# Attention and routed experts in one kernel: a 96-row last tile, casts and routing moved between slots

## The chip, the cores and the metric

The kernel runs on one core of one Trainium2 chip. The metric is the device time of one execution in microseconds, here the median of three runs: 294.62 us (294.39 to 295.03). A profiled execution records every instruction and is longer (span 307.8 us); its times are read as differences and shares. The engines: PE is TensorE (PEld its weight loads), ACT ScalarE, DVE VectorE, POOL GpSimd, SP SyncE, which starts most of the large transfers.

## The reference

First a linear attention without softmax, then a layer of eight experts of which each row uses one:

```python
kv = np.einsum('bhsd,bhse->bhde', k, v)          # 8 batches, 8 heads, 576 rows, 64 wide
out = np.einsum('bhsd,bhde->bhse', q, kv)
rms = np.sqrt(np.mean(out * out, axis=-1, keepdims=True) + 1e-06)
x = out / rms * g_norm                            # -> rows: N = 8*576 = 4608, D = 512

logits = x @ w_gate                               # E = 8
expert_idx = np.argmax(logits, axis=1)
probs = np.exp(logits - logits.max(-1, keepdims=True))
probs /= probs.sum(-1, keepdims=True) + 1e-09
gate_w = probs[np.arange(N), expert_idx]
for e in range(E):
    mask = expert_idx == e
    h = np.maximum(x[mask] @ w1[e], 0.0)          # w1: 512 x 1024
    out[mask] = gate_w[mask, None] * (h @ w2[e])  # w2: 1024 x 512
```

The inputs are one fixed draw of random numbers.

## The kernel before

It has two parts. The attention part goes through 36 tiles (slots 0 to 35) of 128 rows: a transpose of q, a product with the batch pair's kv matrices into `op`, the mean of squares, the scaling into fp16 rows `xg`. The gate is folded into kv: each batch's kv is copied, transposed (`kvt`) and multiplied with the gate's weights (`kgp`), and the result stands as 16 more columns beside kv, so the logits come out of the same product. Every few tiles a `Route` finds each row's expert and its rank there, and GpSimd scatters the rows by expert into a scratch array in HBM. The rows of experts 0 and 1 known after 22 tiles (up to 384 each, AT = 3 tiles) are gathered back early.

The expert part runs one job per expert: gather the rows, transpose them (`flip`), first layer with relu (`one`), second layer (`two`), scale, put the rows to their places. Every expert has room for CAP rows in CT tiles, and rows above are done in left-over tiles of 128, the first of them as a ninth job, more in a loop at the end that runs only if they exist.

All instructions stand in the order of the program text on their engines; each engine works strictly through its own list.

```python
    CT = 5
    CAP = CT * 128
    AT = 3
    NOV = (N - CAP) // 128
    BIG = 1.0e6
...
    c32[:, 144:144 + CT] = ar[:, None] + 128.0 * np.arange(CT)   # rank of each place in an expert
```

The copies, transposes and gate products of a batch's kv, and the casts of the weights to fp16:

```python
        def kv_copy(b):
            for ip in range(2):
                ps = slice(64 * ip, 64 * ip + 64)
                nc.scalar.copy(
                    kvsb[b % 4][ps, :, ps].rearrange("p (c i) n -> p c i n", c=2),
                    kvst[b][ps, :, 0:128].rearrange("p c (i n) -> p c i n", i=2),
                )

        def kv_t(b):
            kvtp = PSA.tile([128, 4, 128], F32, tag="misc", bufs=1, name="kvtp")
            for t in range(4):
                nc.tensor.transpose(kvtp[:, t, :], kvsb[b % 4][:, t, 0:128], ident)
            kvst[b] = PA.tile([128, 4, 128], F32, tag="kvt", bufs=1, name="kvt")
            nc.scalar.copy(kvst[b], kvtp)

        def kv_gate(b):
            kgp = PSA.tile([128, 4, 16], F32, tag="misc", bufs=1, name="kgp")
            for t in range(4):
                nc.tensor.matmul(
                    kgp[:, t, :], kvst[b][:, t, :], gw[:, t, :, :], start=True, stop=True
                )
            nc.vector.tensor_copy(kvsb[b % 4][:, :, 128:144], kgp)
...
        def half1(self, eng, kk):
            ...
            if eng is nc.scalar:
                eng.activation(self.w1[:, kk, :], st, ACTF.Copy, scale=g2)
            ...
        def half2(self, kk, eng=None):
            copy = nc.scalar.copy if eng is None else eng.tensor_copy
            ...
```

One tile's norm. `rest` is called at the slot's end, after the list `late`:

```python
        def x_norm(s, op):
            ...
            nc.scalar.activation(                  # sq = op^2
                sq.rearrange("p (c i h) n -> p c i (h n)", c=2, i=2),
                oc[:, :, :, 0:128], ACTF.Square,
            )
            ms = PA.tile([128, 8], F32, tag="ms", bufs=3, name="ms")
            nc.vector.reduce_sum(ms, sq, axis=AXX)

            def rest():
                ...
                nc.scalar.activation(lnt, ms, ACTF.Ln, scale=1.0 / 64.0, bias=epsb)
                ...
                nc.scalar.activation(rinv, lnt, ACTF.Exp, scale=-0.5)
                ...                                # DVE: lr = op's logits * rinv
                ...                                # DVE: xg = op * rinv, frees op
```

Routing is in pieces (`first_a`: three VectorE instructions lg, mx, dl; `first_b`: cd, m2, oh; `ranks` on TensorE; `send`; `scatter`). What is done in which slot is written in the lists `mid`, `late` and `last`:

```python
        def pace(s):                               # POOL waits here for tile s's logits
            P, g0, G, r = place(s)
            nc.gpsimd.tensor_copy(tick, lrs[P, g0][:, r, 0, 0:1])
...
        for b in range(1, B):
            f = 9 * (b // 2) + 4 * (b % 2)         # first slot that needs batch b
            ...
            at(late, f - 2, kv_copy, b)
            at(mid, f - 1, kv_t, b)
            at(late, f - 1, kv_gate, b)
...
        groups = [(P, g0, G) for P in range(3) for g0, G in ((0, 4), (4, 5))]
        for P, g0, G in groups + [(3, 0, 4), (3, 4, 3)]:
            rt = Route(P, g0, G)
            s = 9 * P + g0 + G - 1
            if P < 3:
                at(late, s + 1, rt.first_a)
                at(late, s + 2, rt.first_b)
                ...
            else:
                at(last, s, rt.first)
                at(mid, s + 2, rt.ranks)
                at(late, s + 2, rt.send)
                for t in range(G):
                    at(last, (33, 34, 34, 35)[t] if g0 == 0 else 35, rt.scatter, t)
                    if g0 == 0 and t == 3:
                        for u in range(AT):
                            at(last, 35, gather_early, 1, u)
        for t in range(AT):
            at(last, 30 + t, gather_early, 0, t)

        at(last, 19, W[0].stage1)
        at(last, 21, W[0].stage2)
        at(last, 30, W[1].stage_in, PA)
        for kk in range(4):
            at(last, (25, 26, 28, 29)[kk], W[0].half1, nc.scalar, kk)
        for kk in range(2):
            at(last, 31 + 2 * kk, W[0].half2, kk)
...
        for s in range(36):
            op = x_mm(s)
            for fn in mid[s]:
                fn()
            if s + 2 < 36:
                qt = x_qt(s + 2)
            elif s == 34:
                ...                                # slot 34: flips of expert 0's early rows
            rest = x_norm(s, op)
            if s + 2 < 36:
                x_qs(s + 2, qt)
            ...
            for fn in late[s]:
                fn()
            rest()
            for fn in last[s]:
                fn()
```

The expert jobs:

```python
        class Job:
            def __init__(self, xe, w, okm, bgm, views):
                ...
                self.nt = nt = len(xe)
                self.cols = nt * 128
                self.halves = 2 if self.cols > 512 else 1
                ...
            def one(self, ws, f):
                ...
                wd = self.cols // self.halves
                ...
                for kk in range(4):
                    nc.tensor.matmul(
                        self.hp[:, f % 2, 0:wd],
                        self.w.w1[:, kk, f * 128:(f + 1) * 128],
                        self.xt[:, kk, ws * wd:(ws + 1) * wd],
                        start=(kk == 0),
                        stop=(kk == 3),
                    )
                if f % 2:
                    r = f % 4 - 1
                    nc.scalar.activation(
                        self.ht[f // 4][:, r:r + 2, ws * wd:(ws + 1) * wd],
                        self.hp[:, :, 0:wd], ACTF.Relu,
                    )

            def two(self, t):
                banks.reverse()
                yp = PSA.tile([128, D], F32, tag=banks[0], bufs=1, name="yp")
                for f in range(8):
                    nc.tensor.matmul(
                        yp, self.ht[f // 4][:, f % 4, t * 128:(t + 1) * 128],
                        self.w.w2[:, f, :], start=(f == 0), stop=(f == 7),
                    )
                spare.append(spare.pop(0))
                ys = PA.tile(
                    [128, D], F32, tag=spare[0], bufs=5 if spare[0] == "qp" else 2, name="ys"
                )
                nc.vector.tensor_scalar(
                    ys, yp, self.xe[t][:, 514:516].bitcast(F32), None, op0=ALU.mult
                )
                put(self.views[t], self.idx[:, t:t + 1], ys)
```

Experts 0 and 1 have three of their tiles done early, so two are left for their jobs; experts 2 to 7 have five. In the loop over jobs, a job's first layer goes together with the casts of the next expert's W1 on VectorE and the flips of the next expert's rows, and its second layer with the casts of the next W2 on ScalarE; each cast frees the staging buffer for the next 2 MB load:

```python
            for ws in range(job.halves):
                for f in range(8):
                    job.one(ws, f)
            ...
                    step = 8 * ws + f
                    if coming and (step in (1, 5, 7, 11, 13) if n > 1 else f in (1, 3, 5, 6, 7)):
                        next_row(n + 2, coming.pop(0), job, ws, f)
                    if ws == job.halves - 1 and f in (2, 4, 6) and flips:
                        nxt.flip(flips.pop(0))
                    if n > 0 and ws == 0 and f % 2 == 1 and nxt is not None:
                        W[n + 1].half1(nc.vector, f // 2)
                        if f == 7 and n + 2 < len(order):
                            W[n + 2].stage1()
            for kk in range(max(job.nt, 4)):
                if kk < job.nt:
                    job.two(kk)
                if n > 0 and kk < (2 if n == 1 else 4) and nxt is not None:
                    W[n + 1].half2(kk)
                if n > 1 and kk == 3 and n + 2 < len(order):
                    W[n + 2].stage2()
```

Of the kernel before, what the change touches and what calls it, by code (L numbers as in the profile page):

```python
# [11 lines left out]
F32 = mybir.dt.float32  # L12
F16 = mybir.dt.float16
I32 = mybir.dt.int32
ALU = mybir.AluOpType
# [13 lines left out]
def kernel(  # L29
# [11 lines left out]
    nc = tc.nc  # L41

    B, H, S, Dh = 8, 8, 576, 64
    N = B * S
# [2 lines left out]
    F = 1024  # L47
    RW = 516
    CT = 5
    CAP = CT * 128  # L50
    AT = 3
    NOV = (N - CAP) // 128
    BIG = 1.0e6

    nc.scalar.add_instruction(
# [19 lines left out]
    c32 = np.zeros((128, 128 + 8 + 8 + CT + 36 + 1 + 32), np.float32)  # L75
    c32[:, 0:128] = np.eye(128)
    c32[:, 128:136] = 8.0 - np.arange(8)
    c32[:, 136:144] = N * np.arange(8)
    c32[:, 144:144 + CT] = ar[:, None] + 128.0 * np.arange(CT)
    o = 144 + CT  # L80
    for s in range(36):
        for c in range(2):
# [59 lines left out]
    class Weights:  # L142
        def __init__(self, e):
            self.e = e if isinstance(e, bass.DynSlice) else slice(e, e + 1)
# [68 lines left out]
    def put(view, idx, ys):  # L213
        nc.gpsimd.indirect_dma_start(  # L214
            out=view,
            out_offset=IndirectOffsetOnAxis(ap=idx, axis=0),
            in_=ys,
            in_offset=None,
            bounds_check=N - 1,
            oob_is_err=False,  # L220
        )
# [4 lines left out]
    W = [Weights(e) if e != "left" else None for e in order]  # L226
# [4 lines left out]
    with tc.manual_schedule(engines=by_hand):  # L231
# [5 lines left out]
        for n in range(4):  # L237
            t = PA.tile([128, 4, 144], F32, tag=f"kvs{n}", name=f"kvs{n}")
# [218 lines left out]
        class Early:  # L457
# [28 lines left out]
            def one(self, m, tag):  # L486

                hp = PSA.tile(
                    [128, 2, 512], F32, tag=tag, bufs=2 if tag == "op" else 1, name="hp"
                )  # L490
                for f in range(2):
                    for kk in range(4):
                        nc.tensor.matmul(  # L493
                            hp[:, f, 0:AT * 128],
                            W[self.e].w1[:, kk, (2 * m + f) * 128:(2 * m + f + 1) * 128],
                            self.xt[:, kk, :], start=(kk == 0), stop=(kk == 3),
                        )
                nc.scalar.activation(
                    self.ht[:, 2 * m:2 * m + 2, :], hp[:, :, 0:AT * 128], ACTF.Relu
                )  # L500

            def two(self, t, yp):
                for f in range(8):
                    nc.tensor.matmul(  # L504
                        yp, self.ht[:, f, t * 128:(t + 1) * 128], W[self.e].w2[:, f, :],
                        start=(f == 0), stop=(f == 7),
                    )
# [95 lines left out]
        late = {s: [] for s in range(36)}  # L603
        last = {s: [] for s in range(36)}

        def at(where, s, fn, *args):
            where[s].append(lambda: fn(*args))

        for b in range(1, B):
            f = 9 * (b // 2) + 4 * (b % 2)  # L610
# [23 lines left out]
# [6 lines that stand above are left out]
                at(mid, s + 3, rt.ranks)  # L640
                at(late, s + 3, rt.send)
                s0 = s + 4 if g0 == 0 else s + 3
                for t in range(G):
                    at(last, s0 + t, pace, s0 + t)
                    at(last, s0 + t, rt.scatter, t)
            else:
                at(last, s, rt.first)
                at(mid, s + 2, rt.ranks)
                at(late, s + 2, rt.send)
                for t in range(G):  # L650
# [4 lines that stand above are left out]
# [4 lines left out]
        at(last, 21, W[0].stage2)  # L659
        at(last, 30, W[1].stage_in, PA)  # L660
        for kk in range(4):
            at(last, (25, 26, 28, 29)[kk], W[0].half1, nc.scalar, kk)
        for kk in range(2):
            at(last, 31 + 2 * kk, W[0].half2, kk)


        load_first()
# [14 lines left out]
        for hh in range(2):  # L682
            ps = slice(64 * hh, 64 * hh + 64)
# [70 lines left out]
        yp = PSA.tile([128, D], F32, tag="misc", bufs=1, name="yp")  # L754
# [11 lines left out]
        yp = PSA.tile([128, D], F32, tag="qtp", bufs=1, name="yp")  # L766
# [16 lines left out]
        def left_over_table():  # L783
# [4 lines left out]
            yield  # L788
            nc.vector.tensor_scalar(ovr, ovr, float(CAP), 0.0, op0=ALU.subtract, op1=ALU.max)
            thr = PA.tile([128, 8, 32], F32, tag="thr")  # L790
# [58 lines left out]
            nc.vector.scalar_tensor_tensor(  # L849
                out=sb, in0=sb, scalar=float(CAP), in1=td, op0=ALU.add, op1=ALU.add  # L850
            )
# [6 lines left out]
        class Job:  # L858


            def __init__(self, xe, w, okm, bgm, views):
                self.xe, self.w, self.okm, self.bgm, self.views = xe, w, okm, bgm, views
                self.nt = nt = len(xe)
                self.cols = nt * 128
                self.halves = 2 if self.cols > 512 else 1
                self.ht = []

# [23 lines left out]
            def one(self, ws, f):  # L891
                if ws == 0 and f % 4 == 0:
                    self.ht.append(PA.tile(
                        [128, 4, self.cols], F16, tag="vq"[f // 4], bufs=2 + f // 4,
                        name="ht",
                    ))
                wd = self.cols // self.halves
                if f % 2 == 0:
                    self.hp = PSA.tile([128, 2, 512], F32, tag="op", bufs=2, name="hp")
# [15 lines that stand above are left out]
            def two(self, t):  # L915
                banks.reverse()
                yp = PSA.tile([128, D], F32, tag=banks[0], bufs=1, name="yp")
                for f in range(8):
                    nc.tensor.matmul(  # L919
                        yp, self.ht[f // 4][:, f % 4, t * 128:(t + 1) * 128],  # L920
                        self.w.w2[:, f, :], start=(f == 0), stop=(f == 7),
                    )
                spare.append(spare.pop(0))
                ys = PA.tile(
                    [128, D], F32, tag=spare[0], bufs=5 if spare[0] == "qp" else 2, name="ys"
                )
                nc.vector.tensor_scalar(  # L927
                    ys, yp, self.xe[t][:, 514:516].bitcast(F32), None, op0=ALU.mult
                )
                put(self.views[t], self.idx[:, t:t + 1], ys)  # L930

        def left_over(t, t0, view):

# [39 lines left out]
        for t in range(AT):  # L973
# [3 lines left out]
            yp = PSA.tile([128, D], F32, tag=banks[0], bufs=1, name="yp")  # L977
# [41 lines left out]

    nov = nc.values_load(tabi[0:1, 1, 7:8], min_val=0, max_val=NOV)  # L1020
    with tc.If(nov > 1):
# [39 lines left out]
```

## Time and profile before

| | |
|---|---|
| time, median of 3 | 294.62 us |
| profiled span | 307.8 us |
| PE busy | 271.7 us (88%) |
| DVE, ACT, POOL busy | 156.5, 158.4, 166.5 us |
| first-layer products (L901) | 480, 67.6 us busy |
| second-layer products (L919) | 280, 62.2 us busy |
| cast w1e on ACT (L178), each | 1.13 us |

The page gives busy time, count and mean duration of each group of instructions, named by line, engine and tile. A product's duration in it includes the way through the array, so products that follow each other closely overlap; their spacing is the cost. The 40 slices give, per slice of 7.7 us, busy tenths of each engine and the clock granted to TensorE. The chain of waits goes back from the last instruction to whatever released it. In a timeline, a bracket at a line's end gives the idle time of the engine before it and who ended it. "issue" is time in which the engine waited for nothing that the profile shows.

The attention part takes until about 128 us of the span, a passage with the early rows of experts 0 and 1 until about 162 us, and the expert jobs the rest. The page also shows places in which nothing seems to move, for instance 136 to 140 us; the profile names no owner for them ("another core or an unknown queue").

### The profile page before, as it was taken

How to read it: one execution, taken by the hardware profiler on the slowest of the kernel's cores; microseconds unless marked ns; L12 is line 12 of the kernel's file. 1: busy time of each engine (PE TensorE's matmuls, PEld its weight loads, DVE VectorE, ACT ScalarE, POOL GpSimd, SP SyncE). 2: the span in 40 equal slices, each digit the busy share in tenths (PEclk: the TensorE clock that was granted, in tenths of full speed). 3: DMA queues.
4: the chain of work that ended last, by engine and by line, in shares of the span. 5: the costliest groups of instructions: out<-in, count | busy, mean ns of one | idle time of the engine just before them, and what ended most of it. 6: DMA issues, size and time to landing. Idle time of an engine off the chain costs nothing.

```text
span 307.8 us, 7171 instructions
## 1 busy us (share of the span) xinstructions
PE 271.7 (88%) x2832; PEld 186.2 (61%) x2832; DVE 156.5 (51%) x422; ACT 158.4 (51%) x295; POOL 166.5 (54%) x243
## 2 busy tenths in 40 slices
PE   8978999989997988475998897799999999999992
PEld 3567887878786967332455554457465574755650
DVE  0024766777686757721713554846354543546130
ACT  1236665766667677525552255355546255472730
POOL 9603226565665547770657687357676675215051
PEclk9999999999999798875999998999999999999998
DMA  7999979969999868230399367999999897978331
GB/s 275 371 389 391 392 229 363 302 252 306 402 399 398 314 197 318 99 92 17 106 363 371 89 230 241 366 344 371 342 351 352 235 403 257 354 288 268 138 117 50
DMA packets 34883, 85.73 MB, mean 279 GB/s; under 512 B 3865, under 2 KB 4125, under 8 KB 34848
## 3 DMA queue, kind: packets, MB, share of 16 engines
q1 hardware_dynamic: 26592, 65.10, 59.2%
q0 software_dynamic: 6976, 18.96, 16.9%
q10 hardware_dynamic: 1280, 1.20, 1.2%
q8 instruction: 23, 0.38, 0.5%
q14 instruction: 12, 0.10, 0.1%
HBM read 71.71 MB, written 15.50 MB: 283 GB/s over the span
## 4 chain that ended last, share of the span: by engine, by line
PE 48%; DMA 13%; issue 13%; ACT 9%; DVE 7%; POOL 5%; another core or an unknown queue 3%; POOLq 1%; SPq 0%
PE hp L901 10%; PE yp L919 10%; PE op L367 9%; DMA out_dram<-ys,idx 7%; PE kvp L298 6%; DMA q<-in_q_dram 4%; PE qtp L345 3%; DMA ws<-in_moe_w_dram 3%; PE hp L493 3%; POOL out_dram L214 2%; PE xp L878 2%; PE yp L504 2%; DVE ms L393 2%; ACT w1e L178 2%
## 5 line engine op out<-in xcount | busy, mean ns | idle before, releaser
L910 ACT ACTIVATE ht<-hp 128x640 f16<-128x640 f32 (+2 forms) x60 | 40.0, 668 | 76.2 <-PE hp L901 67.0
L214 POOL DMA_INDIRECT out_dram<-ys,idx x41 | 42.3, 1032 | 54.3 <-DVE ys L927 43.4
L901 PE MATMUL hp<-xt,w1e 128*128 128x320 f16 (+2 forms) x480 | 67.6, 294 | 2.3 <-issue 2.1
L919 PE MATMUL yp<-w2e,ht 128*128 128x512 f16 x280 | 62.2, 379 | 2.9 <-issue 2.1
L901 PEld LDWEIGHTS <-w1e 128*128 128x128 f16 x480 | 45.4, 99 | 19.1 <-issue 3.0
L927 DVE TENSOR_SCALAR ys<-yp,xe 128x512 f32<-128x512 f32 x35 | 26.2, 751 | 47.0 <-PE yp L919 36.0
L367 PE MATMUL op<-kvs,qts 128*128 128x144 f32 (+1 forms) x320 | 48.0, 306 | 2.2 <-DVE xg L407 1.2
L919 PEld LDWEIGHTS <-ht 128*128 128x128 f16 x280 | 27.2, 98 | 34.8 <-issue 2.8
L590 POOL DMA_INDIRECT xs_scratch<-xg,sli x36 | 35.5, 986 | 22.3 <-issue 22.3
L367 PEld LDWEIGHTS op<-kvs,qts 128*128 128x128 f32 (+1 forms) x320 | 39.2, 185 | 5.7 <-DVE kvs L325 2.0
L197 POOL DMA_INDIRECT xe<-xs_scratch,rowi x34 | 36.1, 1063 | 10.0 <-issue 5.4
L393 DVE TENSOR_REDUCE ms<-sq 128x8 f32<-128x512 f32 x36 | 24.6, 683 | 19.7 <-ACT sq L388 16.0
L388 ACT ACTIVATE sq<-op 128x512 f32<-128x512 f32 x36 | 21.4, 596 | 21.2 <-PE op L367 20.2
L192 ACT CAST w2e<-ws 128x1024 f16<-128x1024 f32 x32 | 31.4, 1040 | 1.5 <-DMA ws<-in_moe_w_dram 1.5
L298 PE MATMUL kvp<-v,k 64*64 64x64 f32 x1152 | 24.6, 226 | 2.0 <-DMA v<-in_v_dram 0.9
L298 PEld LDWEIGHTS kvp<-v,k 64*64 64x64 f32 x1152 | 20.4, 137 | 7.6 <-issue 7.6
L407 DVE TENSOR_TENSOR xg<-op,rinv 128x512 f16<-128x512 f32 x36 | 24.5, 681 | 0.0
L281 POOL COPY qp<-q 128x512 f32<-128x512 f32 x32 | 19.3, 615 | 9.4 <-DMA q<-in_q_dram 9.3
L345 PE MATMUL qtp<-cf,qp 128*128 128x128 f32 x144 | 23.1, 284 | 1.2 <-POOL qp L281 1.2
L352 ACT COPY qts<-qtp 128x512 f32<-128x512 f32 x36 | 21.1, 585 | 6.1 <-PE qtp L345 6.0
L180 DVE TENSOR_SCALAR w1e<-ws,g 128x1024 f16<-128x1024 f32 x29 | 20.9, 756 | 5.7 <-DMA ws<-in_moe_w_dram 5.7
L882 DVE COPY xt<-xp 128x512 f16<-128x512 f16 x35 | 13.5, 418 | 19.1 <-PE xp L878 17.6
(115 smaller groups left out, 275.9 us busy)
## 6 DMA issues: line engine op xcount, KB each, us to landing
ws<-in_moe_w_dram SPq DMA_DIRECT2D x16, 2048.0 KB
q<-in_q_dram SPq DMA_DIRECT2D x8, 1152.0 KB
k<-in_k_dram SPq DMA_DIRECT2D x7, 1152.0 KB
v<-in_v_dram SPq DMA_DIRECT2D x7, 1152.0 KB
ws<-in_moe_w_dram SPq DMA_DIRECT2D x4, 1024.0 KB
k<-in_k_dram SPq DMA_DIRECT2D x2, 576.0 KB
v<-in_v_dram ACTq DMA_DIRECT2D x2, 576.0 KB
out_dram<-ys,idx POOLq DMA_INDIRECT x41
```

The lines of the kernel that those rows point to most:

```text
L192: copy(self.w2[:, 2 * kk:2 * kk + 2, :], self.s2[:, 2 * kk:2 * kk + 2, :])
L197: return nc.gpsimd.indirect_dma_start(out=xe.bitcast(I32), out_offset=None, in_=xs.ap() if src is None else src, in_offset=IndirectOffsetO ...
L214: nc.gpsimd.indirect_dma_start(out=view, out_offset=IndirectOffsetOnAxis(ap=idx, axis=0), in_=ys, in_offset=None, bounds_check=N - 1, oob_ ...
L298: nc.tensor.matmul(kvst[b][64 * ip:64 * ip + 64, c, 64 * i2:64 * i2 + 64], ld["k", b][ps, i, cs], ld["v", b][ps, i, cs], start=(j == 0), s ...
L345: nc.tensor.transpose(qtp[:, c, i2, :], qp[s][:, c, 2 * i2:2 * i2 + 2, :], ident)
L367: nc.tensor.matmul(op[ts, c, 144 * i2:144 * i2 + 144], qts[s][:, 2 * i2 + c, ts], kvs[:, 2 * c + i2, :], start=True, stop=True,)
L393: nc.vector.reduce_sum(ms, sq, axis=AXX)
L590: put_xs = nc.gpsimd.indirect_dma_start(out=xs_views[9 * self.P + self.g0 + t], out_offset=IndirectOffsetOnAxis(ap=self.sli[:, t:t + 1], a ...
L901: nc.tensor.matmul(self.hp[:, f % 2, 0:wd], self.w.w1[:, kk, f * 128:(f + 1) * 128], self.xt[:, kk, ws * wd:(ws + 1) * wd], start=(kk == 0 ...
L910: nc.scalar.activation(self.ht[f // 4][:, r:r + 2, ws * wd:(ws + 1) * wd], self.hp[:, :, 0:wd], ACTF.Relu,)
L919: nc.tensor.matmul(yp, self.ht[f // 4][:, f % 4, t * 128:(t + 1) * 128], self.w.w2[:, f, :], start=(f == 0), stop=(f == 7),)
L927: nc.vector.tensor_scalar(ys, yp, self.xe[t][:, 514:516].bitcast(F32), None, op0=ALU.mult)
```

## The change

Three things are changed.

- The fifth tile of an expert has 96 rows instead of 128 (LT = 96), so CAP falls from 640 to 608 rows. The first layer's moving operand is 608 columns wide in two halves of 304 instead of 320; for experts 0 and 1, which have two tiles left, 224 instead of 256. In the second layer, the result scaling and the put, the last tile has 96 rows. The places from row 96 of the fifth tile get a rank of 1e7, so that no row belongs to them. More rows of a full expert go to a left-over tile.
- The four casts of expert 0's W1 on ScalarE go from the ends of slots 25, 26, 28 and 29 to those of slots 26, 27, 28 and 30. Batches 6 and 7 have their kv transposed in the middle of slots 26 and 30, and the copy of the result on ScalarE stood behind the casts of slots 25 and 29. The second cast of its W2 goes from slot 33 to slot 32.
- The first routing step of tiles 27 to 30, and of 31 to 33, is done in two pieces: `first_a` at the end of the slot, `first_b` one slot later, behind the next tile's reduction, as the earlier groups already do it.

```diff
--- before.py
+++ after.py
@@ -47,9 +47,10 @@
     F = 1024
     RW = 516
     CT = 5
-    CAP = CT * 128
+    LT = 96
+    CAP = (CT - 1) * 128 + LT
     AT = 3
-    NOV = (N - CAP) // 128
+    NOV = -(-(N - CAP) // 128)
     BIG = 1.0e6
 
     nc.scalar.add_instruction(
@@ -77,6 +78,7 @@
     c32[:, 128:136] = 8.0 - np.arange(8)
     c32[:, 136:144] = N * np.arange(8)
     c32[:, 144:144 + CT] = ar[:, None] + 128.0 * np.arange(CT)
+    c32[LT:, 144 + CT - 1] = 1.0e7
     o = 144 + CT
     for s in range(36):
         for c in range(2):
@@ -644,7 +646,8 @@
                     at(last, s0 + t, pace, s0 + t)
                     at(last, s0 + t, rt.scatter, t)
             else:
-                at(last, s, rt.first)
+                at(last, s, rt.first_a)
+                at(late, s + 1, rt.first_b)
                 at(mid, s + 2, rt.ranks)
                 at(late, s + 2, rt.send)
                 for t in range(G):
@@ -659,9 +662,9 @@
         at(last, 21, W[0].stage2)
         at(last, 30, W[1].stage_in, PA)
         for kk in range(4):
-            at(last, (25, 26, 28, 29)[kk], W[0].half1, nc.scalar, kk)
+            at(last, (26, 27, 28, 30)[kk], W[0].half1, nc.scalar, kk)
         for kk in range(2):
-            at(last, 31 + 2 * kk, W[0].half2, kk)
+            at(last, 31 + kk, W[0].half2, kk)
 
 
         load_first()
@@ -861,7 +864,8 @@
             def __init__(self, xe, w, okm, bgm, views):
                 self.xe, self.w, self.okm, self.bgm, self.views = xe, w, okm, bgm, views
                 self.nt = nt = len(xe)
-                self.cols = nt * 128
+                self.rows = [128] * nt if nt == 1 else [128] * (nt - 1) + [LT]
+                self.cols = sum(self.rows)
                 self.halves = 2 if self.cols > 512 else 1
                 self.ht = []
 
@@ -891,7 +895,7 @@
             def one(self, ws, f):
                 if ws == 0 and f % 4 == 0:
                     self.ht.append(PA.tile(
-                        [128, 4, self.cols], F16, tag="vq"[f // 4], bufs=2 + f // 4,
+                        [128, 4, self.nt * 128], F16, tag="vq"[f // 4], bufs=2 + f // 4,
                         name="ht",
                     ))
                 wd = self.cols // self.halves
@@ -915,9 +919,11 @@
             def two(self, t):
                 banks.reverse()
                 yp = PSA.tile([128, D], F32, tag=banks[0], bufs=1, name="yp")
+                ps = slice(0, self.rows[t])
                 for f in range(8):
                     nc.tensor.matmul(
-                        yp, self.ht[f // 4][:, f % 4, t * 128:(t + 1) * 128],
+                        yp[ps, :],
+                        self.ht[f // 4][:, f % 4, t * 128:t * 128 + self.rows[t]],
                         self.w.w2[:, f, :], start=(f == 0), stop=(f == 7),
                     )
                 spare.append(spare.pop(0))
@@ -925,9 +931,10 @@
                     [128, D], F32, tag=spare[0], bufs=5 if spare[0] == "qp" else 2, name="ys"
                 )
                 nc.vector.tensor_scalar(
-                    ys, yp, self.xe[t][:, 514:516].bitcast(F32), None, op0=ALU.mult
-                )
-                put(self.views[t], self.idx[:, t:t + 1], ys)
+                    ys[ps, :], yp[ps, :], self.xe[t][ps, 514:516].bitcast(F32), None,
+                    op0=ALU.mult,
+                )
+                put(self.views[t], self.idx[ps, t:t + 1], ys[ps, :])
 
         def left_over(t, t0, view):
```

## The prediction

> **What bounds the kernel now.** I read the page's busy table and 40 slices first, then the chain of waits that ended last, then the timeline from 88 to 200 us and the windows of the expert stage. All times inside the profiled execution (span 307.8 us) are used only as differences; the predicted time starts from the timed median, 294.62 us.
>
> The chain, from tile 26 of the attention part:
>
> ```profile
> 96.63 1.13 ACT w1e L178
> 97.79 0.58 ACT kvt L317
> 98.38 0.51 ACT sq L388
> 98.91 0.69 DVE ms L393
> 99.81 1.25 PE op L367 x8
> ...
> 110.80 1.04 ACT w1e L178
> 111.86 0.58 ACT kvt L317
> ...
> 179.65 8.45 DMA ws<-in_moe_w_dram
> ...
> 224.72 5.98 PE hp L901 x44
> 230.70 0.45 PE xp L878 x8
> 231.15 1.09 PE hp L901 x8
> ```
>
> The columns are start, duration, and what. Three stages are to be seen. Around 96 and 110 us a cast of expert 0's W1 (w1e) stands on ScalarE in front of the small copy kvt, and TensorE waits for kvt before it can do the gate products kgp and the next tile. At 180 us a 2 MB weight load is the limit. From about 197 us on the chain is TensorE alone: 40 second-layer products, 64 first-layer products, the transposes, again and again.
>
> The timeline shows how much the casts cost, with the same place in an earlier batch (no cast in it) for comparison:
>
> ```profile
> 42.70 0.58 ACT L317 COPY kvt<-kvtp 128x512 f32<-128x512 f32 x1 [0.21 <-PE kvtp L315]
> 43.34 1.06 PE L322 MATMUL kgp<-gw,kvt 128*128 128x16 f32 x8 [0.24 <-ACT kvt L317]
> ...
> 96.21 0.66 PE L315 MATMUL kvtp<-cf,kvs 128*128 128x128 f32 x4 [0.64 <-ACT kvs L307]
> ...
> 98.43 1.06 PE L322 MATMUL kgp<-gw,kvt 128*128 128x16 f32 x8 [1.12 <-ACT kvt L317]
> ...
> 112.50 1.06 PE L322 MATMUL kgp<-gw,kvt 128*128 128x16 f32 x8 [1.12 <-ACT kvt L317]
> ```
>
> The brackets give the idle time before and who ended it: 1.12 us twice with the cast, 0.24 us without.
>
> What the rest of the attention part hangs on is GpSimd's queue (copy "tick" waits for a tile's logits, then a scatter of rows, then a gather for expert 0):
>
> ```profile
> 114.63 0.19 POOL L626 COPY tick<-lr 128x1 f32<-128x1 f32 x1 [1.16 <-DVE lr L401]
> 118.37 0.19 POOL L626 COPY tick<-lr 128x1 f32<-128x1 f32 x1
> 123.44 1.04 POOL L197 DMA_INDIRECT xe<-xs_scratch,rowa  x1 [0.31 <-issue]
> 126.21 0.40 PE L469 MATMUL xp<-ch,xe 128*128 128x128 f16 x4 [2.14 <-DMA xe<-xs_scratch,rowa]
> ```
>
> From tile 30's tick at 114.63 on, no tick waits: the queue is full until the third gather ends at 124.48, and TensorE stands 2.14 us for that gather's data before it can do tile 35 behind it in its queue.
>
> In the windows of the expert stage (one expert each; busy times, then granted clock, DMA share, GB/s) TensorE is busy throughout:
>
> ```profile
> 197.37:215.93 18.56, 18.56 (x127) 11.16 (x124) 11.19 (x31) 9.51 (x12) 11.75 (x14) 1.00 1.00 365
> 253.51:271.98 18.47, 18.47 (x127) 11.15 (x125) 9.02 (x21) 9.39 (x12) 6.50 (x8) 1.00 0.88 325
> ```
>
> **What the Trainium skill says.** "TensorE: Matmul & The Clock Gate", section "Wait — 56ns, not 53.3ns?": a warm matmul costs its columns at 2.4 GHz plus about 2.5 ns. The trace agrees: 40 products of 512 columns in 8.63 us are 215.8 ns each, 8 of 320 in 1.09 us are 136 ns. Same page, "The HAM clock gate": TensorE's clock halves after a window of little activity. The trace agrees in kind: the slices show granted clocks of 7 or 8 tenths near 100 and 115 us, right after the two kgp waits, and the eight op products of tile 28 take 1.94 us instead of 1.25. Same page, "Weight-path perf modes": the fast weight load is for 128 columns of a type other than fp32, so the 96-wide last tile would lose it. Here fp16 loads of 128 columns last 98 ns and the fp32 loads of L367, 185 ns; nothing in this trace shows a 96-wide load.
>
> **The change, part by part.**
>
> *1. The fifth tile has 96 rows.* A full expert's first layer goes from 2 x 320 to 2 x 304 columns. From 215.8 ns at 512 and 136.2 ns at 320 a column costs 0.415 ns, so 16 fewer are 6.6 ns; times 64 products that is 0.42 us per expert. Experts 3 to 7 (five) run with TensorE full: 2.1 us. Expert 2 ends behind the 8.45 us load, the casts that wait for it and the transposes behind those on VectorE, so I give it 0.1. Experts 0 and 1 have two tiles left here, 256 to 224 columns, 32 products, again 0.42 us each; expert 1's stretch is full on VectorE (174.11 to 179.62: four w1e, five xt copies, place rows), so 0; expert 0 I give half, 0.2. Second layer: the 96 rows are the stationary operand, the 512 moving columns stay, so nothing. The result scaling on VectorE (0.75 us) runs over 512 elements in each partition either way: nothing. The relu on ScalarE (0.70 us) gets some 5% shorter, under TensorE anyway. GpSimd's put may get shorter, and has idle time. Sum: 2.4 us.
>
> *2. Casts moved from slots 25, 26, 28, 29 to 26, 27, 28, 30.* kvt for tile 27's batch can start at 96.21 + 0.66 = 96.87 instead of 97.79, and that for the next at 110.95 instead of 111.86: 0.92 and 0.91; compared with the earlier batch 1.12 - 0.24 = 0.88 each. I take 0.88 x 2 = 1.8 us. The moved casts land where ScalarE waits: slot 27's fits into the 2.00 us in which ScalarE waits for tile 28's products; slot 30's (1.13 us) about fits before tile 31's.
> With shorter kgp waits the first half-clock window (tiles 27 to 29) may not occur: the earlier batches have the same pattern and full clock. Tiles 27 to 29 take 3.20 + 3.51 = 6.71 us from op to op; the same tiles nine earlier, 2.36 + 3.97 = 6.33. So 0.4, which I round to 0.5 us since tile 30 gains a little too. The second window falls after 114.7, where GpSimd's queue limits, and is worth nothing.
>
> *3. Second W2 cast from slot 33 to 32; routing of tiles 27 to 30 (and 31 to 33) in two pieces.* The second piece, three VectorE instructions (about 0.65 us), now stands behind the next tile's reduction and fills the 0.6 us in which VectorE waits for ScalarE's Ln and Exp; tile 31's reduction starts some 0.6 us sooner. The cast in slot 32 delays tile 33's square by about 1 us. Both happen while GpSimd's full queue sets the time, and the flip wait of 2.14 us swallows them: 0, within 0.3 either way.
>
> Sum: 2.4 + 1.8 + 0.5 = 4.7 us, so 294.6 - 4.7 = 289.9 us.
>
> **The rivals.**
>
> *The GpSimd queue absorbs the slots.* For: from 114.63 on it is full. Against: at tile 30 it waited 1.16 us for the logits, at tile 29 1.65 us, so tile 30's tick moves with the logits, and all gains of part 2 lie before it. Were they absorbed, only part 1 remains: about 292.2.
>
> *The slow weight load shows.* If the 96-wide loads cost on TensorE's path, say the 0.09 us by which fp32 loads are longer than fp16, times 8 loads in 8 experts, 5.8 us would go and the kernel would be about even or 1 us slower. Against: the fp32 loads of L367 lie behind products spaced only 0.12 us apart, the new ones behind products 0.216 us apart.
>
> *DMA takes over.* For: share 1.00 in expert 3's window. Against: by the packets the weights for expert 4's first layer land 1.5 us before their cast, later ones 1.8 to 4.5 us; 0.42 us per expert does not use that up.
>
> *Overflow.* Computed with the reference, the experts get 564, 494, 600, 572, 539, 654, 585 and 600 rows. Above 640 lies expert 5 with 14, above 608 expert 5 with 46: one left-over tile in both. For experts 0 and 1 unused early places count too (353 and 301 of 384 used): 595 and 577, still below 608. Were a second left-over tile needed, the loop at the end would run with its own weight loads (8 us and more each) and the kernel would pass 305.
>
> *More clock comes back.* TensorE's half-clock windows at 128 to 135, 138 to 145 and 190 us may shift or vanish; each full window is worth up to 1.7 us. This could bring 288, or cost as much if a window lands worse.
>
> **Range and chances.** Parts 1 and 2 without clock give 290.4; absorbed slots 292.2; a clock window more 288.2. I take 289.9 with 287.9 to 292.3. Faster by over 2% needs 5.9 us or more, below 288.7, which wants an extra clock window: 0.20. Slower by over 2% would need overflow or something not seen: 0.03. Within 2%: 0.77.
>
> **What would show it.** Period of experts 4 to 7 down from 18.47 to about 18.05 us, products of 304 columns at 129.6 ns, 512-column products still 216 ns with 96-wide loads; both kgp waits down to about 0.24 us; tile 30's tick earlier by about 2.3 us relative to tile 26, and the flip wait for the third gather still there; clock of 1.00 at 101 to 104 us. I am wrong if the period stays at 18.47, if second-layer products before a 96-wide tile stretch, if the kgp wait has another owner, or if the left-over loop runs.

## The result, and the profile after

The changed kernel takes 290.58 us (median of 6, 289.61 to 291.85) where the kernel before, beside it, takes 294.50 us (median of 6): ratio 0.9863, 95% interval 0.9831 to 0.9895, so 4.0 us less (3.1 to 5.0). In a second measurement the ratio was 0.9834 (0.9806 to 0.9863). Predicted were 289.9 us and 4.7 us less, within 2%.

The profiled span, though, fell from 307.8 to 289.0 us. Most of that is no effect of the change: the kernel before, profiled a second time, has a span of 294.4 us (the first experiment). That second profile is the one to compare with from here on. Nor is an execution longer for being profiled, as was taken ahead of the prediction: the profiled one of the changed kernel took 290.84 us, where the median of its six is 290.58. Lines have moved: L901, L919 and L878 of the kernel before are L905, L924 and L882 after.

The page of the changed kernel; the clock slices now hold one dip near 118 us and one from 173 to 188 us:

```profile
span 289.0 us, 7171 instructions
...
PEclk9999999999999999799999996899999999999999
...
L905 PE MATMUL hp<-xt,w1e 128*128 128x304 f16 (+2 forms) x480 | 64.2, 287 | 0.3 <-ACT ht L914 0.2
```

The timeline of the changed kernel at the places of the two casts and of GpSimd's queue:

```profile
93.88 1.06 PE L324 MATMUL kgp<-gw,kvt 128*128 128x16 f32 x8 [0.24 <-ACT kvt L319]
...
105.40 1.06 PE L324 MATMUL kgp<-gw,kvt 128*128 128x16 f32 x8 [0.24 <-ACT kvt L319]
...
107.53 0.19 POOL L628 COPY tick<-lr 128x1 f32<-128x1 f32 x1 [0.28 <-DVE lr L403]
...
116.31 0.40 PE L471 MATMUL xp<-ch,xe 128*128 128x128 f16 x4 [0.95 <-DMA xe<-xs_scratch,rowa]
117.89 1.29 PE L471 MATMUL xp<-ch,xe 128*128 128x128 f16 x8 [1.18 <-DMA xe<-xs_scratch,rowa]
```

Both kgp waits are 0.24 us, as in the earlier batches. Tile 30's tick still waits for its logits, but only 0.28 us (1.16 before), so GpSimd's queue just kept up. TensorE still waits for the gathers before tile 35.

The chain of waits of the changed kernel, one expert of the last stage:

```profile
208.64 5.68 PE hp L905 x44
214.32 0.45 PE xp L882 x8
214.77 1.03 PE hp L905 x8
215.80 0.51 PE xp L882 x8
216.32 1.03 PE hp L905 x8
217.35 0.29 PE xp L882 x4
...
226.79 5.68 PE hp L905 x44
```

The next expert begins 18.15 us after this one; in the second profile of the kernel before it is 18.47. 44 products of 304 columns take 5.68 us, 129.1 ns each; before, 44 of 320 took 5.98. But the second flip shows 0.51 us here, and the first 0.45: it stands a little.

The stage that did not give is expert 2, here in the timeline and in two windows (busy times of PE, PEld, DVE, ACT, POOL, then clock, DMA share, GB/s) of the changed kernel:

```profile
169.92 0.75 DVE L182 TENSOR_SCALAR w1e<-ws,g 128x1024 f16<-128x1024 f32 x1 [5.17 <-DMA ws<-in_moe_w_dram]
...
176.61 1.01 PE L882 MATMUL xp<-ch,xe 128*128 128x128 f16 x8 [5.44 <-DVE xt L886]
```

```profile
171.00:176.60 5.60, 0.17 (x2) 0.02 (x1) 5.46 (x16) 0.37 (x1) 4.31 (x6) 0.92 0.93 332
176.60:183.00 6.40, 6.39 (x31) 3.80 (x32) 2.96 (x12) 2.55 (x4) 1.21 (x2) 0.54 1.04 399
```

VectorE waits 5.17 us for expert 3's W1, then casts it; the copy of expert 2's flip stands behind these casts in its queue, and TensorE does 0.17 us of work in 5.6 us. After that it works at a granted clock of 0.54 for 6.4 us.

### The profile page after: what moved, and what is told of

Read it like the earlier page. It is cut to its first block, busy times and chain, and to the rows that moved or that the text cites. A ratio compares the mean times of both kernels' runs of the same rounds, so it can differ in the third digit from the quotient of the medians.

```text
span 289.0 us, 7171 instructions
## 1 busy us (share of the span) xinstructions
PE 261.6 (91%) x2832; PEld 184.9 (64%) x2832; DVE 157.4 (54%) x422; ACT 156.0 (54%) x295; POOL 166.8 (58%) x243
## 4 chain that ended last, share of the span: by engine, by line
PE 23%; DMA 14%; issue 9%; POOL 6%; DVE 4%; POOLq 1%
PE yp L924 10%; PE hp L905 10%; DMA out_dram<-ys,idx 8%; POOL out_dram L216 3%; DMA ws<-in_moe_w_dram 3%; DMA xe<-xs_scratch,rowi 2%; PE xp L882 2%; POOL xe L199 2%; DVE w1e L182 2%; POOL xs_scratch L592 1%; DMA xs_scratch<-xg,sli 1%; DVE xt L886 1%; POOLq L1063 0%; DVE idx L210 0%; POOLq L216 0%
## 5 line engine op out<-in xcount | busy, mean ns | idle before, releaser
L914 ACT ACTIVATE ht<-hp 128x608 f16<-128x608 f32 (+2 forms) x60 | 38.3, 640 | 75.6 <-PE hp L905 69.8
L905 PE MATMUL hp<-xt,w1e 128*128 128x304 f16 (+2 forms) x480 | 64.2, 287 | 0.3 <-ACT ht L914 0.2
L924 PE MATMUL yp<-w2e,ht 128*128 128x512 f16 (+1 forms) x280 | 62.7, 382 | 0.0
L905 PEld LDWEIGHTS <-w1e 128*128 128x128 f16 x480 | 45.4, 99 | 13.8 <-issue 0.6
L933 DVE TENSOR_SCALAR ys<-yp,xe 128x512 f32<-128x512 f32 (+1 forms) x35 | 26.2, 750 | 44.4 <-PE yp L924 43.4
L369 PE MATMUL op<-kvs,qts 128*128 128x144 f32 (+1 forms) x320 | 47.1, 302 | 2.0 <-DVE xg L409 1.0
L924 PEld LDWEIGHTS <-ht 128*128 128x128 f16 (+1 forms) x280 | 29.2, 104 | 30.7 <-issue 1.1
L369 PEld LDWEIGHTS op<-kvs,qts 128*128 128x128 f32 (+1 forms) x320 | 38.5, 182 | 5.4 <-DVE kvs L327 2.0
L199 POOL DMA_INDIRECT xe<-xs_scratch,rowi x34 | 36.9, 1085 | 8.4 <-issue 4.5
L395 DVE TENSOR_REDUCE ms<-sq 128x8 f32<-128x512 f32 x36 | 24.6, 684 | 14.9 <-ACT sq L390 14.1
L300 PE MATMUL kvp<-v,k 64*64 64x64 f32 x1152 | 23.0, 223 | 0.8 <-DMA v<-in_v_dram 0.8
L347 PE MATMUL qtp<-cf,qp 128*128 128x128 f32 x144 | 22.3, 276 | 1.5 <-POOL qp L283 1.5
L886 DVE COPY xt<-xp 128x512 f16<-128x512 f16 x35 | 13.5, 419 | 18.1 <-PE xp L882 16.2
L300 PEld LDWEIGHTS kvp<-v,k 64*64 64x64 f32 x1152 | 19.4, 134 | 5.8 <-issue 5.8
```

Source lines behind the costliest of these rows:

```text
L199: return nc.gpsimd.indirect_dma_start(out=xe.bitcast(I32), out_offset=None, in_=xs.ap() if src is None else src, in_offset=IndirectOffsetO ...
L300: nc.tensor.matmul(kvst[b][64 * ip:64 * ip + 64, c, 64 * i2:64 * i2 + 64], ld["k", b][ps, i, cs], ld["v", b][ps, i, cs], start=(j == 0), s ...
L369: nc.tensor.matmul(op[ts, c, 144 * i2:144 * i2 + 144], qts[s][:, 2 * i2 + c, ts], kvs[:, 2 * c + i2, :], start=True, stop=True,)
L905: nc.tensor.matmul(self.hp[:, f % 2, 0:wd], self.w.w1[:, kk, f * 128:(f + 1) * 128], self.xt[:, kk, ws * wd:(ws + 1) * wd], start=(kk == 0 ...
L914: nc.scalar.activation(self.ht[f // 4][:, r:r + 2, ws * wd:(ws + 1) * wd], self.hp[:, :, 0:wd], ACTF.Relu,)
L924: nc.tensor.matmul(yp[ps, :], self.ht[f // 4][:, f % 4, t * 128:t * 128 + self.rows[t]], self.w.w2[:, f, :], start=(f == 0), stop=(f == 7),)
```

## The experiments

**The kernel before, profiled again.** No edit.

> The kernel before, profiled a second time, because its first profile (span 307.8 us against 294.5 us timed) stands still in places that the profile of the changed kernel (289.0 us) does not have. If the stops belong to that one execution, the second span is 292 to 296 us, the stretch from tile 35 to the weight loads of expert 2 is some 8 to 10 us shorter than in the first, and both kgp waits are again about 1.12 us. If they belong to the kernel before, the span is again about 307 us and the change removed them.

Span 294.4 us. From tile 35 to expert 0's first product it takes 28.5 us, in the first profile 36.4: the stops belonged to that one execution. The waits that the prediction was built on are there again. Timeline of this second profile of the kernel before:

```profile
94.91 1.06 PE L322 MATMUL kgp<-gw,kvt 128*128 128x16 f32 x8 [1.12 <-ACT kvt L317]
...
108.58 1.06 PE L322 MATMUL kgp<-gw,kvt 128*128 128x16 f32 x8 [1.03 <-ACT kvt L317]
```

and its list of waits around expert 2 shows that the long wait there is no work of the change (waiter, releaser, us in total, times, longest):

```profile
PE xp L878 <- DVE xt L882: 5.1, 1, 5.1
DVE w1e L180 <- DMA ws<-in_moe_w_dram: 5.0, 1, 5.0
```

**The 96-row tile alone.** The changed kernel, with

```diff
-                at(last, s, rt.first_a)
-                at(late, s + 1, rt.first_b)
+                at(last, s, rt.first)
-            at(last, (26, 27, 28, 30)[kk], W[0].half1, nc.scalar, kk)
+            at(last, (25, 26, 28, 29)[kk], W[0].half1, nc.scalar, kk)
-            at(last, 31 + kk, W[0].half2, kk)
+            at(last, 31 + 2 * kk, W[0].half2, kk)
```

> Only the 96-row last tile; casts and routing as before. By the prediction's part 1: 2.4 us less than before, ratio 0.992. By the rival that the wait of expert 2 for the 2 MB load takes in what experts 0 and 1 gain and a longer wait there halves TensorE's clock once more: 1.0 to 1.5 us less, ratio 0.995 to 0.997. By the rival of the slow 96-wide weight load: no gain or slower.

Ratio 0.9942 (0.9919 to 0.9964): 1.7 us less (1.1 to 2.4 of 295.7). That lies between the first two expectations, and the predicted 2.4 at the interval's edge; no gain, as the rival of the slow weight load has it, is ruled out. Its profile says where: from expert 3's first product to that of the ninth job it takes 89.7 us against 91.4, 1.7 us less; from the start of expert 3's W1 load to expert 3's first product 28.2 us against 28.8, with half-clock windows in both. The second difference is no gain of the rows: the same stretch takes 29.0 us in the first profile of the changed kernel.

**The casts alone.** The kernel before, with `(25, 26, 28, 29)` of `half1` made `(26, 27, 28, 30)`.

> Only the four casts of expert 0's W1 moved to slots 26, 27, 28 and 30. By the prediction's part 2: 1.8 us from the two waits and 0.5 us from the clock, 2.3 us less, ratio 0.992. If the GpSimd queue or the later wait for the load absorbs the gain: under 0.5 us. If all of the change's 4 us came from here and the rows gave nothing: 4 us, ratio 0.986.

Ratio 0.9951 (0.9931 to 0.9971): 1.4 us less (0.9 to 2.0). The two waits, 1.8 us, lie inside the interval; with the clock's 0.5 they do not. In the profiles the waits are 0.24 us, and tile 26 to tile 31 takes 14.92 us, in every profile with the new slots 14.9. With the old slots it is 16.6 us where no half-clock window falls into it (two profiles) and 18.0 and 19.2 us where one does (two profiles). Tiles 26 and 31 in the timeline of the 96-row tile alone, which has the old slots, and then in that of the casts alone:

```profile
91.30 1.25 PE L369 MATMUL op<-kvs,qts 128*128 128x144 f32 x8
...
107.92 1.99 PE L369 MATMUL op<-kvs,qts 128*64 128x144 f32 x16
```

```profile
91.45 1.25 PE L367 MATMUL op<-kvs,qts 128*128 128x144 f32 x8
...
106.37 1.58 PE L367 MATMUL op<-kvs,qts 128*64 128x144 f32 x16
```

The gain goes on through GpSimd's queue: tile 26 to tile 35 takes 29.4 and 29.0 us in the two profiles with the old slots and no half-clock window before tile 31, 27.9 here, and 27.1 to 27.6 in the changed kernel and its variants.

**Routing and the W2 cast alone.** The kernel before, with `31 + kk` and `rt.first` in its two pieces.

> Only the routing in two pieces and the second W2 cast in slot 32. By the prediction's part 3: 0 within 0.3 us, ratio 0.999 to 1.001, since GpSimd's queue sets the time there. By the rival that VectorE's order matters once the casts are in their old slots: 0.6 us less.

Ratio 1.0000 (0.9976 to 1.0024): no effect that can be measured, as predicted; an effect of 0.6 us lies within the interval and is not ruled out. In the traces there is one. GpSimd's queue, second profile of the kernel before, then this run, at the tick of tile 31 and the scatter behind it:

```profile
114.45 0.19 POOL L626 COPY tick<-lr 128x1 f32<-128x1 f32 x1
115.14 1.04 POOL L590 DMA_INDIRECT xs_scratch<-xg,sli  x1 [0.50 <-issue]
```

```profile
113.43 0.18 POOL L626 COPY tick<-lr 128x1 f32<-128x1 f32 x1
113.77 1.04 POOL L590 DMA_INDIRECT xs_scratch<-xg,sli  x1 [0.16 <-issue]
```

The scatter follows 0.3 us sooner, and so does the next one: from tile 30's tick to tile 33's it takes 9.8 to 9.9 us in the four profiles with the routing in one piece, 9.15 to 9.2 in the ten with two. So the queue was not full, though the prediction read it so from its ticks. The likely reason, argued and not tested, is that the scatter waits for the rows xg that it sends: VectorE ends tile 31's at 114.99 us in the first timeline, after the tick, and at 113.56 in the second, before the tick's end. Whether these 0.6 us reach the end of the kernel is not shown.

**112 and 88 rows.** The changed kernel with `LT = 112` and with `LT = 88`.

> The changed kernel with 112 rows in the last tile (halves of 312 columns). If the columns of the first layer set the gain, 16 of 32 fewer columns per expert keep half of part 1: about 1.2 us slower than the changed kernel, ratio to before about 0.990 to 0.991. If only the step from 128 matters (or 96 rows cost a slow weight load), this is as fast as the changed kernel or faster.

> The changed kernel with 88 rows (halves of 300; the largest regular experts have exactly 600 rows, so still one left-over tile). If the columns set the gain: 4 columns per product times 0.415 ns times 64 times five experts, 0.5 us faster than the changed kernel, ratio about 0.984 to 0.985. If the puts of 88 rows spread worse over the DMA engines and that shows: slower than the changed kernel by 1 us or more.

| rows in the last tile | period of experts 3 to 6, us | saved per period | 64 products' columns would save | ratio to before |
|---|---|---|---|---|
| 128 | 18.47 | | | |
| 112 | 18.31 | 0.16 | 0.21 | 0.9856 (0.9813 to 0.9899) |
| 96 | 18.15 | 0.32 | 0.43 | 0.9863, 0.9834 |
| 88 | 18.07 | 0.40 | 0.53 | 0.9807 (0.9759 to 0.9854) |

The fourth column is columns saved times 0.415 ns times 64. The timed ratios cannot tell the three apart (112 rows came out a little faster than expected), but the period, the same in each of four experts of a profile, can: the gain follows the columns, and it is three quarters of what 64 products would give. There is no step at 128 and no penalty at 88. The weight load behind it, by shape, in the changed kernel:

```profile
L924 PEld LDWEIGHTS <-ht 128*128 128x128 f16 x216 | 21.3, 99 | 24.5 <-issue 1.1
...
L924 PE MATMUL yp<-w2e,ht 128*96 128x512 f16 x64 | 15.1, 379 | 0.0
...
L924 PEld LDWEIGHTS <-ht 128*96 128x96 f16 x64 | 7.9, 123 | 6.1
```

The 96-wide loads are longer than the 128-wide ones, 123 against 99 ns, and cost nothing: no idle time stands before their products, which last 379 ns and, from expert 3 on, start 216 ns apart like those of 128.

**Where a quarter of the columns went: the flips' spacing.** Timeline of the kernel before (second profile), then of the changed kernel, in the same expert:

```profile
255.72 0.61 PE L878 MATMUL xp<-ch,xe 128*128 128x128 f16 x8
...
256.37 0.76 DVE L882 COPY xt<-xp 128x512 f16<-128x512 f16 x2 [2.98 <-PE xp L878]
...
257.27 0.61 PE L878 MATMUL xp<-ch,xe 128*128 128x128 f16 x8
```

```profile
250.46 0.61 PE L882 MATMUL xp<-ch,xe 128*128 128x128 f16 x8
...
251.11 0.76 DVE L886 COPY xt<-xp 128x512 f16<-128x512 f16 x2 [2.70 <-PE xp L882]
...
252.01 0.61 PE L882 MATMUL xp<-ch,xe 128*128 128x128 f16 x8
```

Flip to flip is 1.55 us in both: 0.65 until the copy starts, 0.76 for it, 0.14 until TensorE goes on. The flips share one PSUM buffer. The eight products in between are hidden behind that, in both kernels, and two such groups are 16 of the 64 products. The 48 others at 6.7 ns are 0.32 us. The test was to put 12 products between flips, in the changed kernel:

```diff
-                    if ws == job.halves - 1 and f in (2, 4, 6) and flips:
+                    if ws == job.halves - 1 and f in (1, 4, 7) and flips:
```

> The changed kernel with the next expert's flips after first-layer groups 1, 4 and 7 instead of 2, 4 and 6. In the profiles of before and after, flip to flip is 1.55 us in both, although the 8 products between them got 0.05 us shorter: the flip waits for VectorE's copy of the one before. If that is where 0.11 of the 0.43 us per expert went, 12 products between two flips take the copy in: period 18.15 down to about 17.95 to 18.05 us, 0.5 to 1 us less in all. If it is something else, 18.15 stays.

The period falls to 18.02 us, so this is where the missing part was. The time does not show it: ratio 0.9849 (0.9804 to 0.9895), beside 0.9834 for the changed kernel in the same comparison; 0.5 us is below what these runs resolve.

**The changed kernel again**, as the reference in that comparison.

> The changed kernel once more, as the reference for the three beside it and as a second profile of it: ratio to before 0.983 to 0.990. Expert period 18.15 us again; if the wait in expert 2 belongs to the kernel and not to one execution, again over 4 us of TensorE waiting for the xt copy there, with at least one half-clock window behind it.

Ratio 0.9834 (0.9806 to 0.9863), period 18.15 us, and TensorE waits 5.8 us in expert 2. What differs between the two profiles is the clock: by the trace's clock record this execution had half clock for 10.2 us from 117 us and for 3.4 us in expert 2, the first one 3.4 and 6.8 us.

**Expert 3's load started earlier.** In the changed kernel, expert 2's W1 casts on VectorE moved from expert 1's first layer (`n > 0` becomes `n > 1` there) to before expert 0's second layer:

```diff
+            if n == 0:
+                for kk in range(4):
+                    W[2].half1(nc.vector, kk)
+                W[3].stage1()
             for kk in range(max(job.nt, 4)):
```

> The changed kernel, with the four casts of expert 2's W1 on VectorE moved from expert 1's first layer to before expert 0's second layer, and with them the start of expert 3's 2 MB load (161.3 us in the profile of the changed kernel). In that profile TensorE waits 5.44 us in expert 2 behind this load and then runs 6.8 us at half clock. If the load's start is the cause: it starts about 6 us earlier, the wait shrinks to under 1 us and the half-clock windows vanish; 4 to 7 us less than the changed kernel, ratio to before 0.963 to 0.973. If the loads then only collide with the gathers, or expert 3's W2 load becomes the wait: under 1.5 us less.

Ratio 0.9826 (0.9779 to 0.9873): the expected gain did not come. The long wait in expert 2 is gone (one half-clock window of 3.4 us is left), but two others came, both named in the second expectation: 3.1 us in expert 1 for gathered rows, and expert 3 takes 20.95 us instead of 18.15, since the start of its W2 load (174.7 us) was still tied to casts in expert 2. The next version moves these too, all four into expert 1's second layer:

```diff
-                    if n == 2 and ws == 0 and f in (3, 7):
-                        W[2].half2(2 + f // 4)
-                        if f == 7:
-                            W[3].stage2()
...
-                if n > 0 and kk < (2 if n == 1 else 4) and nxt is not None:
+                if n > 0 and kk < 4 and nxt is not None:
                     W[n + 1].half2(kk)
-                if n > 1 and kk == 3 and n + 2 < len(order):
+                if n > 0 and kk == 3 and n + 2 < len(order):
```

> As the kernel before in this list, and with all four casts of expert 2's W2 in expert 1's second layer, so that expert 3's W2 load too starts some 4 us earlier. If W2's landing is the next wait: 0.5 to 2 us less than without it. If not: the same within 0.5 us.

Ratio 0.9734 (0.9692 to 0.9775), by the medians 2.4 us less than without it, more than the 2 expected at most. Expert 3 is back at 18.15 us. What is left, in this version's timeline of expert 1:

```profile
158.35 0.38 PE L882 MATMUL xp<-ch,xe 128*128 128x128 f16 x4 [0.17 <-DVE xt L886]
161.78 0.40 PE L882 MATMUL xp<-ch,xe 128*128 128x128 f16 x4 [3.04 <-DMA xe<-xs_scratch,rowi]
```

The load (started at 155.2 us) now runs beside expert 2's gathers, and half a flip waits for its rows. Two more versions hold the load's start back until expert 1's first flip is copied, the second with the flips at 1, 4 and 7 as well:

```diff
-                W[3].stage1()
...
+                    if n == 1 and f == 2:
+                        W[3].stage1(hold=True)
```

> The version with expert 2's casts early, but the start of expert 3's W1 load held back until expert 1's first flip is copied. In the version before it TensorE waited 3.04 us in expert 1 for expert 2's gathered rows, which share the DMA engines with that load. If the load delays the gathers: this wait falls below 1 us, expert 1's period from 13.4 to about 10 us, and 1 to 3 us are gained, ratio to before 0.963 to 0.970. If the gathers are late by themselves (their issue on GpSimd), the wait stays, and the load's later arrival makes it the same or 1 us slower.

> The last one with the flips after groups 1, 4 and 7 as well: another 0.5 us less if the flips' spacing is a cost of its own; the same if the first flip in expert 1 now comes before its rows have landed.

Ratios 0.9654 (0.9605 to 0.9703) and 0.9691 (0.9661 to 0.9722). All ratios in this document leave out executions that took over 1.5% longer than the fastest of their kernel, and for the first of these two versions that is four of six: the median of all six is 288.75 us beside 296.02, a ratio of 0.975, so that it is not shown to be faster than the version before it. The second is faster than the kernel before by over 2%; between these two there is no verdict. In the profiles the stretch from expert 0's first product to expert 3's takes 42.8 and 41.8 us in the changed kernel, 39.1 and 39.4 in the first two versions and 38.5 and 38.4 in these: holding the load back gains about 1 us, and most of the 3 us wait has only moved.

The wait for the gathers has gone from the flips of expert 1, whose period falls from 13.5 to 8.3 and 7.6 us (with the flips at 1, 4 and 7, one of 1.2 us appears in expert 0 instead), and the load is again what expert 2 waits for, in the second version's timeline:

```profile
159.56 0.61 PE L882 MATMUL xp<-ch,xe 128*128 128x128 f16 x8
...
169.19 0.75 DVE L182 TENSOR_SCALAR w1e<-ws,g 128x1024 f16<-128x1024 f32 x1 [3.08 <-DMA ws<-in_moe_w_dram]
...
175.07 1.01 PE L882 MATMUL xp<-ch,xe 128*128 128x128 f16 x8 [2.91 <-DVE idx L210]
```

TensorE waits 2.9 us for VectorE, which had waited for the load, instead of 5.4 to 5.8. That the gathers were late because of the load, and not by themselves, follows from the same gathers being in time once the load starts 4.5 us later.

## Why the prediction was right or wrong

The sum was right: 4.7 us predicted, 4.0 (3.1 to 5.0) measured, and 0.9834 is inside the range as well. That the whole came so near may be luck in part, since its steps, timed alone, make 3.1. By its steps:

- *1, columns.* A product got 6.8 ns shorter (5.98 to 5.68 us for 44) where 6.6 were predicted. The term mis-sized is the count: 64 products per expert were taken as all on TensorE's path, but 16 of them lie between flips whose spacing VectorE's copy sets. Experts 3 to 7 gave 1.7 us (91.4 to 89.7) where 2.1 were predicted; the last of them has one flip only, so nothing is hidden there, and gave its full 0.43. Experts 0 and 1, put at 0.2 together, gave 0.2 to 0.6: expert 3's load starts 13.8 to 14.0 us after expert 0's first product in three profiles with 96 rows, 14.2 to 14.4 in three with 128. Expert 1, put at nothing because VectorE looked full there, takes 8.43 us instead of 8.59. Of expert 2, which ends at that load, no gain can be seen. By the profiles step 1 is then 1.9 to 2.3 us, by the time 1.7 (1.1 to 2.4), of 2.4 predicted.
- *1, what was put at nothing.* The 96-wide loads, the scaling and the puts: right. VectorE's scaling takes 747 ns for 96 rows and 751 for 128.
- *2, the waits.* Right: 1.12 to 0.24 us, and 16.6 to 14.9 us from tile 26 to tile 31. Timed alone 1.4 us (0.9 to 2.0), where 1.8 were predicted.
- *2, the clock.* Mis-sized, on a reference that was itself disturbed. The stretch nine tiles earlier (6.33 us) contains 3.97 us from tile 19 to tile 20, which takes 2.87 in the second profile. Tiles 27 to 29 take 5.23 us without a half-clock window (the 96-row tile alone) and 6.71 with one, in both profiles of the kernel before: 1.5 us, not 0.4. The window appears in two of four profiles with the old slots and in none of ten with the new, which fits the mechanism and does not prove it. In the time the 0.5 us is not shown: 2.3 us for the casts lies outside the interval, and the mean granted clock rose only from 0.9705 (51 executions of the kernel before) to 0.9722 (22 with the casts moved), by estimate 0.3 of a window of 3.4 us.
- *3, routing and W2.* Nothing measurable in the time, as predicted, but the reason was wrong: GpSimd's queue was not full, and became 0.6 us shorter. That this does not show in the time is not explained; here the prediction may have been lucky.
- *The rivals.* GpSimd's queue did not absorb the slots, with 0.28 us to spare at tile 30. The slow weight load exists (123 against 99 ns) and stays hidden. DMA did not take over: from expert 3's first product on, no cast of the changed kernel waits for a load. No overflow loop ran.

1.7 and 1.4 and 0 make 3.1 us, the whole is 4.0 and in the second measurement 4.9; the intervals overlap, and whether the parts help one another stays open. Some of it is the clock. Of the 51 executions of the kernel before, the 19 with a mean granted clock of 0.976 or 0.977 have a median of 294.93 us, the 16 with 0.965 to 0.967 one of 296.33. By estimate (the lost clock over 294 us, at half of 3.4 us a window) these differ by 1.9 windows, so about 0.7 us each. The profiles with the new slots agree: from tile 26 to expert 0's first product they take 56.0 and 56.7 us with 3.4 us of half clock, 56.8 to 57.2 with 6.8 (three), 57.7 to 58.4 with 10.2 (five). In the second measurement the changed kernel had a mean clock of 0.975 and the kernel before 0.969, one window less, so some 0.7 of the 4.9 us. Whether a window costs this by itself, or comes with idle time that costs it, was not separated.

## What to carry to other kernels

Before multiplying a saving per instruction by their number, see which of them lie between two events whose spacing another engine sets: here a fixed flip-to-flip time of 1.55 us in two profiles took a quarter. A stage that ends at a load takes in what is saved while the load is under way, and keeps what is saved before the load starts; look for what starts that load, and move that, then look at once at what the load now runs beside. One profile can hold stops that the next does not have; profile twice before explaining a gap.

## What was not expected of the hardware

- The first profile of the kernel before has 13 us that the second does not have, 8 of them between tile 35 and expert 0's job, with no releaser in the trace.
- The prediction named the Trainium skill's "TensorE: Matmul & The Clock Gate" for the clock. By the trace's clock record the half-clock times are about 3.4, 6.8 or 10.2 us long, and the same kernel has different ones in two executions (3.4 and 6.8 us in one, 10.2 and 3.4 in the other). The 3.4 us ahead of the windows near tile 28 were not idle: TensorE was busy for 2.3 and 2.2 us of them in the two profiles of the kernel before. The 51 executions of the kernel before run from 293.56 to 298.31 us, 1.6%, more than any of the steps is worth.
- Same page, "Weight-path perf modes": the fast load is only for 128 columns. Measured: 123 ns for 96 columns, 99 for 128, and behind products 216 ns apart it cost nothing.
